# Layer 1's second product over token blocks of 512, 384, 384 and 512, with two small reorderings

## The chip, the core and the metric

The kernel runs on one core of a Trainium2 chip. The metric is device time in microseconds (us), the median of three runs. PE is TensorE's matmul, PEld its weight load, DVE is VectorE, ACT ScalarE, POOL GpSimd, SP SyncE; SPq and ACTq are instructions that issue a DMA from SP's and ACT's queue.

## The reference

Attention with a sigmoid in place of the softmax, then two feed-forward layers, all in float32 with 1792 tokens, model width 768 and inner width 2048:

```python
scores = scale * np.matmul(q, k.transpose(0, 1, 3, 2)) - np.log(S)      # q, k, v: (4, 12, 448, 64)
x = np.matmul(1.0 / (1.0 + np.exp(-scores)), v)                         # reshaped to (1792, 768)
h = x @ w_in;   x = (h * (1.0 / (1.0 + np.exp(-h)))) @ w_out            # layer 1
h = x @ w_in2                                                           # layer 2
P = a[0] + a[1] * h + a[2] * h2 + a[3] * h3
Q = 1.0 + np.abs(b[0]) * np.abs(h) + np.abs(b[1]) * h2
out = (P / (Q + 1e-06)) @ w_out2
```

The weights come as float64 arrays, seen as pairs of int32.

## The kernel before

Everything is written in a fixed order by hand (`manual_schedule`): each engine executes its instructions in the order in which the Python code issues them. A `Ring` is a first-in, first-out list of buffers, and a buffer that is taken again makes its new writer wait for the last reader.

Every float32 operand of a matmul is split in two parts, high and low (`split`, `split2`): ACT casts the high part (L365, L369), DVE subtracts it from the operand (L366, L370). A product of two split operands is three matmuls: high by high, high by low, low by high.

The program has these stages. (1) Attention, to about 172 us. (2) Layer 1's first product with seven products in place of eight (p1 to p7, all matmuls in `product`, L501), to about 375 us; its results pass through SiLU (`silu`) and are stored to DRAM in `gd`. (3) Layer 1's second product, `second(n)`, from 375 to 616 us. (4) Layer 2's first product (`first2`, L709 to L711), over token blocks of 512, 384, 512, 384 in the turn 0, 2, 1, 3, to about 848 us. (5) Layer 2's second product with seven products (`second2`, L902) and their sums (`evict`), to the end.

Stage 3 is what the change is about. The tokens lie along the moving operand. There are four blocks of 448 tokens (b) and 16 chunks of 128 inner rows (c); n = 16 b + c. `second(n)` issues 18 matmuls (L637, L638, L639): for each of six 128-wide output tiles d, three matmuls into one PSUM bank, with `woH[c]`, `woH[c]`, `woL[c]` as weights and the high, low, high part of `gx[n]` as moving operand. `woH[0]`, `woL[0]`, `woH[1]`, `woL[1]` lie in four tiles that the trace calls w; the others are woH and woL. `gx[n]` is one of six split buffers, all in the tile `xa_all`, 2 x 448 elements each. In front of the matmuls of n stand `load_g(n + 4)`, a DMA on ACT's queue that reads `gd` (L603), and behind them `load_wo1(n + 5)` (L618, also ACT's queue), `split_wo1(n + 2)` and `split_gd(n + 2)`. `load_wo1` has four buffers (`wos`), `load_g` takes one of nine buffers of 448 (`f448`), which also serve the results.

After c = 15 `results1(b)` copies the six banks to SBUF, three on ACT, three on DVE (L645), and SP stores them to `xs[1]` (L646). There are eight banks: block b + 1 begins in the two that block b has not used. Between all this stand the conversions of layer 2's weights (`conv`, one ACT and four DVE instructions, a load of 768 KB and a store of 384 KB on SP's queue), whose number up to each n is set by `conv_by`.

At the border of stages 2 and 3 (g == last) the code interleaves the last products p5, p3, p7 with `split_wo1(0)`, `load_wo1(4)`, `split_gd(0)`, then `split_wo1(1)`, `load_wo1(5)`, `split_gd(1)`; `both(g - 1, "r", "c")` is a DVE addition (L387) that reads a PSUM bank which `second(0)` then takes over.

In stage 5 each of the seven products ends with seven tiles of 128 tokens x 384 in PSUM, which `evict(k_, i)` adds up. For k_ == 1 the sum goes to one of three spare buffers (`ores`) and is stored to the output by SP (L957). PSUM tiles hold two banks each: hp2 holds the bank of tile 3 and that of tile 4.

## Time and profile before

| what | value |
|---|---|
| three runs | 1066.99, 1069.32, 1070.0 us; median 1069.32 |
| the profiled execution | 1066.57 us; span of its instructions 1064.8 us |
| mean granted TensorE clock | 0.998 |
| PE, DVE, ACT, POOL busy | 1052.4, 761.1, 605.5, 250.1 us of the span |
| DMA | 255.80 MB, 239 GB/s over the span |
| stage 3, first matmul of n = 0 to first of layer 2 | 375.14 to about 616.1 us |

The profile is of one execution. A busy time is the union of the instructions' durations; matmuls overlap, so the pace of PE is read from the starts of its instructions in the order of time, not from their durations. An idle time in square brackets stands before the instruction it is printed with, and the arrow names what ended it.

### The profile page before, as it was taken

Reading aid. Unit: us, or ns where it says so; the run is one execution under the profiler, and the core shown is the slowest. Engines: PE = TensorE matmul, PEld = TensorE weight load, DVE = VectorE, ACT = ScalarE, POOL = GpSimd, SP = SyncE. Lnnn points to the kernel's source line nnn. Section 1 sums busy time; section 2 is a strip of 40 time slices with the busy share of each in tenths; the row PEclk is TensorE's granted clock in tenths of the full one; section 3 lists DMA queues with packets and bytes.
Section 4 is the critical chain, followed back from the end, with each engine's and each line's share of the span. In section 5 each row is a group of like instructions: output and inputs, shape, how many; then the busy total and the mean of one; then the engine's idle time right before and its main releaser. Section 6 shows DMA issues by size and latency. Waiting matters only on the chain.

```text
span 1064.8 us, 16177 instructions
## 1 busy us (share of the span) xinstructions
PE 1052.4 (99%) x5654; PEld 915.5 (86%) x5654; DVE 761.1 (71%) x1084; ACT 605.5 (57%) x911; POOL 250.1 (23%) x203
## 2 busy tenths in 40 slices
PE   8999999999999999999999999999999999999998
PEld 5555556999999989999999988888999998999997
DVE  3678877888987757595967328879897977445761
ACT  5778886656755554333334258676778866354430
POOL 2112210000000000000002256768968921300000
PEclk9999999999999999999999999999999999999999
DMA  8998877777566788597998334656788879866651
GB/s 231 272 287 236 247 248 244 255 248 254 197 232 220 262 275 281 191 375 280 359 334 303 109 127 136 221 191 223 248 275 300 286 238 314 271 227 198 207 157 53
DMA packets 152338, 255.80 MB, mean 240 GB/s; under 512 B 13888, under 2 KB 109760, under 8 KB 152256
## 3 DMA queue, kind: packets, MB, share of 16 engines
q1 hardware_dynamic: 139968, 233.23, 67.3%
q10 hardware_dynamic: 12224, 21.53, 6.2%
q8 instruction: 44, 0.72, 0.3%
q14 instruction: 38, 0.31, 0.1%
q0 software_dynamic: 64, 0.00, 0.0%
HBM read 168.53 MB, written 86.18 MB: 239 GB/s over the span
## 4 chain that ended last, share of the span: by engine, by line
PE 80%; DVE 6%; POOL 5%; DMA 3%; ACT 2%; issue 2%; SPq 0%; ACTq 0%; DVEq 0%; POOLq 0%
PE acc L501 14%; PE hp L902 13%; PE hb L342 6%; PE pair L318 6%; PE acc L639 6%; PE acc L638 6%; PE acc L637 6%; PE hb L501 5%; PE hb L902 5%; PE hp L709 2%; PE hp L710 2%; PE hp L711 2%; POOL sb L829 2%; PE hb L637 2%; PE hb L639 2%
## 5 line engine op out<-in xcount | busy, mean ns | idle before, releaser
L370 POOL TENSOR_TENSOR w<-wif,w 128x768 fp32r<-128x768 f32 x2 | 4.0, 2034 | 427.1 <-DMA wif<-w1i 427.1
L333 ACT ACTIVATE sb<-pair,nls 128x896 f32<-128x896 f32 x84 | 81.1, 1008 | 33.6 <-PE pair L318 33.5
L639 PE MATMUL acc<-xa_all,woL 128*128 128x448 f32 x252 | 92.7, 368 | 0.0
L637 PE MATMUL acc<-xa_all,woH 128*128 128x448 f32 x252 | 92.7, 368 | 0.0
L638 PE MATMUL acc<-xa_all,woH 128*128 128x448 f32 x252 | 92.7, 368 | 0.0
L190 ACT ACTIVATE sb<-sb 128x768 f32<-128x768 f32 x64 | 58.0, 907 | 55.4 <-DMA sb<-in_moe_w_out_dram 27.2
L738 POOL TENSOR_TENSOR sb<-sb 128x1024 f32<-128x1024 f32 (+1 forms) x32 | 70.1, 2190 | 37.1 <-ACT sb L735 37.1
L342 PE MATMUL hb<-sb,vs 128*64 128x448 f32 (+1 forms) x384 | 73.9, 554 | 0.1
L501 PE MATMUL acc<-xb,wr 128*128 128x448 f32 x315 | 67.7, 366 | 0.0
L829 POOL TENSOR_TENSOR sb<-sb 128x384 f32<-128x384 f32 (+1 forms) x43 | 51.0, 1194 | 60.3 <-DMA sb<-gk 58.4
L501 PEld LDWEIGHTS acc<-xb,wr 128*128 128x128 f32 x315 | 59.1, 188 | 5.4 <-issue 0.7
L196 DVE SCALAR_TENSOR_TENSOR sb<-sb 128x768 int32<-128x768 int32 x64 | 61.9, 967 | 2.2
L193 DVE SCALAR_TENSOR_TENSOR sb<-sb 128x768 int32<-128x768 int32 x64 | 61.6, 963 | 2.2
L709 PE MATMUL hp<-hx,woH 128*128 128x512 f32 (+1 forms) x168 | 61.6, 367 | 0.0
L710 PE MATMUL hp<-hx,woH 128*128 128x512 f32 (+1 forms) x168 | 61.6, 367 | 0.0
L711 PE MATMUL hp<-hx,woL 128*128 128x512 f32 (+1 forms) x168 | 61.6, 367 | 0.0
L709 PE MATMUL hp<-xa_all,woH 128*128 128x512 f32 (+1 forms) x168 | 60.7, 362 | 0.0
L711 PE MATMUL hp<-xa_all,woL 128*128 128x512 f32 (+1 forms) x168 | 60.7, 362 | 0.0
L710 PE MATMUL hp<-xa_all,woH 128*128 128x512 f32 (+1 forms) x168 | 60.7, 362 | 0.0
L740 DVE TENSOR_TENSOR sb<-hp,sb 128x768 f32<-128x768 f32 (+1 forms) x31 | 33.6, 1084 | 35.2 <-ACT sb L737 35.2
L318 PEld LDWEIGHTS pair<-xa_all 64*128 64x128 f32 x384 | 34.7, 190 | 24.8 <-issue 12.3
L366 DVE TENSOR_TENSOR xa_all<-sb,xa_all 128x448 fp32r<-128x448 f32 x67 | 45.0, 681 | 10.9 <-ACT xa_all L365 10.8
(239 smaller groups left out, 2769.1 us busy)
## 6 DMA issues: line engine op xcount, KB each, us to landing
sb<-in_moe_w_in_dram SPq DMA_DIRECT2D x32, 768.0 KB, 6.9
sb<-in_moe_w_out_dram SPq DMA_DIRECT2D x32, 768.0 KB, 6.4
gd<-sb SPq DMA_DIRECT2D x64, 224.0 KB, 3.2
sb<-gd ACTq DMA_DIRECT2D x64, 224.0 KB, 4.7
wf<-w0i SPq DMA_DIRECT2D x32, 384.0 KB, 3.7
gk<-sb SPq DMA_DIRECT2D x27, 384.0 KB, 3.9
xs<-sb SPq DMA_DIRECT2D x36, 224.0 KB, 2.8
gk<-sb SPq DMA_DIRECT2D x15, 512.0 KB, 3.1
```

The lines of the kernel that those rows point to most:

```text
L318: nc.tensor.matmul(p[:, j, :S], K[rows[j], a_, c * P : (c + 1) * P], Q[rows[j], b_, :], start=(n == 0), stop=(n == len(turns) - 1),)
L333: nc.scalar.activation(t, p[:, :, :S], AF.Sigmoid, bias=nls, scale=QKSCALE)
L342: nc.tensor.matmul(hb[i_ % 2][j * D : (j + 1) * D, :S], vs[i_][part, j, c * D : (c + 1) * D], t[part, j], start=(c == 0), stop=(c == LAST),)
L501: nc.tensor.matmul(o, w_[:, w], x[:, i_, :], start=first and kk == 0 and n_ == 0, stop=kk == HK - 1 and n_ == 2, skip_group_check=not first,)
L637: nc.tensor.matmul(o, woH[c][:, w], x[:, 0, :], start=(c == 0), stop=False)
L638: nc.tensor.matmul(o, woH[c][:, w], x[:, 1, :], start=False, stop=False)
L639: nc.tensor.matmul(o, woL[c][:, w], x[:, 0, :], start=False, stop=(c == KF - 1))
L709: nc.tensor.matmul(o, wh[:, w], x[:, 0, :wd_], start=first, stop=False)
L710: nc.tensor.matmul(o, wh[:, w], x[:, 1, :wd_], start=False, stop=False)
L711: nc.tensor.matmul(o, wl[:, w], x[:, 0, :wd_], start=False, stop=last)
L829: nc.gpsimd.tensor_tensor(out=o, in0=i0, in1=i1, op=op)
L902: nc.tensor.matmul(o, a_, y[:, w_, :], start=kk == 0 and n_ == 0, stop=kk == HF - 1 and n_ == 2)
```

## The change

The four blocks of `second` become 512, 384, 384 and 512 tokens wide (`YW`, `YB`), cut out of `gd` tiles that now hold all 1792 tokens of a chunk. The number of matmuls stays: 1152. The split buffers (`hg`) are 2 x 512 elements each, six of them, still in `xa_all` and at its start; the fourth to sixth get free at different times. The loads of `gd` have a ring of their own (`fg`): first five buffers used once (`once`: three of `xio`, two halves of the fifth split buffer), then five (three in `xa_all`, two in `f_all`), three of which are given up in the last block (`late`) for others of the results' ring. The results' ring (`fr`) has five buffers, two to five in the last block. From n = 11 on, loads and splits of `gd` go one product further ahead. `load_wo1(4)`, `(5)` and `(6)` are issued one product later; `load_g(5)` and `(6)` after the first results of n = 2; one load more before. The conversions begin to go faster at n = 10 instead of 16 and are spread by columns instead of products. In layer 2, `evict` for k_ == 1 writes its sum to `w_`, a buffer per tile that is next written for k_ == 4; `ores` is gone.

```diff
-    gd = [[dr_p.tile([P, S], F32, tag=f"gd{c}_{b}", name=f"gd{c}_{b}") for b in range(B)] for c in range(KF)]
+    gd = [dr_p.tile([P, NT], F32, tag=f"gd{c}", name=f"gd{c}") for c in range(KF)]
...
+    YW = (BK, BK - P, BK - P, BK)
+    YB = [(sum(YW[:i]), w) for i, w in enumerate(YW)]
+    fg, fr, hg = Ring([]), Ring([]), Ring([])
+    once, late = [], []
...
     def load_g(n):
         if n < B * KF:
             b, c = divmod(n, KF)
-            gq[n] = f448.get()
-            nc.scalar.dma_start(out=gq[n], in_=gd[c][b])
+            c0, w = YB[b]
+            gq[n] = fg.get()
+            nc.scalar.dma_start(out=gq[n][:, :w], in_=gd[c][:, c0 : c0 + w])
...
-            nc.tensor.matmul(o, woH[c][:, w], x[:, 0, :], start=(c == 0), stop=False)
+            nc.tensor.matmul(o, woH[c][:, w], x[:, 0, :w_], start=(c == 0), stop=False)
...
     def results1(b):
+        c0, w = YB[b]
         for d in range(KD):
-            t = f448.get()
+            t = fr.get()
...
         elif k_ == 1:
-            o = ores.get()
-            add(o, ps, s_)
-            store(0, 0, i, o)
-            ores.put(o)
+            add(w_, ps, s_)
+            store(0, 0, i, w_)
...
-        hl = Ring(xa[:6])
+        xp = [xa_all[:, i * 2 * BK : (i + 1) * 2 * BK].rearrange("p (j s) -> p j s", j=2) for i in range(6)]
+        hg.put(*xp[:4])
...
             if g == last:
-                for n in range(4):
+                once.extend([*xio.free, *(xp[4][:, j].bitcast(F32) for j in range(2))])
+                fg.put(*once)
+                for n in range(5):
                     load_g(n)
...
                 split_wo1(0)
-                load_wo1(4)
                 split_gd(0)
...
                 split_wo1(1)
-                load_wo1(5)
                 split_gd(1)
+                load_wo1(4)
...
         split_wo1(2)
-        load_wo1(6)
+        hg.put(xp[5])
+        xf32 = [xa_all[:, (12 + i) * BK : (13 + i) * BK].bitcast(F32) for i in range(3)]
+        fg.put(*xf32)
         split_gd(2)
-        load_g(4)
-        load_g(5)
+        load_wo1(5)
...
+        knee = KF - 6
         def conv_by(n):
-            if n <= KF:
+            if n <= knee:
                 return first + (n - 1) // 4
...
         for n in range(2, NL1):
-            load_g(n + 4)
+            more_by = 1 if n > 2 * KF // 3 else 0
+            if n > 2:
+                load_g(n + 4 + more_by)
...
             if n == 2:
                 c21(last)
                 both(last, "r", "c")
                 c12(last)
...
                 split_wo1(3)
                 split_gd(3)
+                load_wo1(6)
+                load_g(5)
+                load_g(6)
...
-            split_gd(n + 2)
+            split_gd(n + 2 + more_by)
...
+            if n == NL1 - KF:
+                late.extend(xf32)
...
+                fg.put(fr.get(), fr.get(), fr.get())
```

The order on the engines moves at three places of stage 3, all on ACT, whose queue also issues the loads of `gd` (L603, now L611) and of W_out (L618, now L630). The first is the border of stages 2 and 3, where L369 (now L370) is the cast of W_out's chunks 0 and 1, and L365 (now L366) that of `gx[0]` and `gx[1]`. Before:

```order
L375 CAST wq_1876<-wf_1_262 128x384
L369 CAST w_1988<-wos_3521 128x768
L618 DMA wos_3521<-w0o_146 128x768
L365 CAST xa_all<-sb 128x448
L369 CAST w_1990<-wos_3522 128x768
L618 DMA wos_3522<-w0o_148 128x768
L365 CAST xa_all<-sb 128x448
```

and now:

```order
L376 CAST wq_1828<-wf_1_214 128x384
L370 CAST w_1940<-wos_3473 128x768
L366 CAST xa_all<-sb 128x512
L370 CAST w_1942<-wos_3474 128x768
L366 CAST xa_all<-sb 128x512
L630 DMA wos_3473<-w0o_98 128x768
L376 CAST wq_1826<-sf_216 128x384
```

The load of chunk 4, which takes the buffer of chunk 0 and so waits for its split, no longer stands in front of the cast of `gx[0]`. The second place is n = 2, where the two L520 (now L521) are the last SiLUs of stage 2. Before:

```order
L618 DMA wos_3523<-w0o_150 128x768
L365 CAST xa_all<-sb 128x448
L603 DMA sb<-gd_0_89 128x448
L603 DMA sb<-gd_0_93 128x448
L603 DMA sb<-gd_0_97 128x448
L520 ACTIVATE sb<-acc_2004 128x448
L520 ACTIVATE sb<-sb 128x448
L369 CAST woH_3717<-wos_3524 128x768
L365 CAST xa_all<-sb 128x448
L618 DMA wos_3524<-w0o_152 128x768
L369 CAST woH_3719<-wos_3521 128x768
```

and now:

```order
L366 CAST xa_all<-sb 128x512
L630 DMA wos_3474<-w0o_100 128x768
L521 ACTIVATE sb<-acc_1956 128x448
L521 ACTIVATE sb<-sb 128x448
L370 CAST woH_3669<-wos_3476 128x768
L366 CAST xa_all<-xa_all 128x512
L630 DMA wos_3475<-w0o_102 128x768
L611 DMA xa_all<-gd_78 128x512
L611 DMA xa_all<-gd_79 128x512
L630 DMA wos_3476<-w0o_104 128x768
L370 CAST woH_3671<-wos_3473 128x768
```

Three loads (two of `gd`, one of W_out) have moved from ahead of the SiLUs to behind the casts of chunk 3, in front of the cast of W_out's chunk 4. The third place is the end of block 0, where L645 (now L658) are ACT's copies of the results. Before:

```order
L190 ACTIVATE sb<-sb 128x768
L603 DMA sb<-gd_1_82 128x448
L365 CAST xa_all<-sb 128x448
L603 DMA sb<-gd_1_86 128x448
L365 CAST xa_all<-sb 128x448
L645 COPY sb<-hb 128x448
```

and now:

```order
L191 ACTIVATE sb<-sb 128x768
L611 DMA sb<-gd_76 128x384
L366 CAST xa_all<-xa_all 128x384
L191 ACTIVATE sb<-sb 128x768
L611 DMA xa_all<-gd_77 128x384
L366 CAST xa_all<-sb 128x384
L658 COPY sb<-hb 128x512
```

Three casts of block 1 (c = 0, 1, 2) stand ahead of the copies where two stood, and so do four conversions (L190, now L191) where one stood.

## Rows read from the trace of the kernel before

**Rows 1.** Page, part 1: engine, busy us (share of the span), instructions.

```profile
PE 1052.4 (99%) x5654; PEld 915.5 (86%) x5654; DVE 761.1 (71%) x1084; ACT 605.5 (57%) x911; POOL 250.1 (23%) x203
```

**Rows 2.** Waits of PE: who waited for whom, us in total, times, longest.

```profile
PE hp L902 <- DVE sb L387: 2.6, 1, 2.6
```

**Rows 3.** Timeline of PE, stage 3: start us, us, instruction; pairs 36 matmuls apart.

```profile
404.75 0.37 PE L637 MATMUL hb<-xa_all,woH 128*128 128x448 f32 x1
...
412.19 0.37 PE L637 MATMUL hb<-xa_all,woH 128*128 128x448 f32 x1
...
438.23 0.36 PE L637 MATMUL acc<-xa_all,w 128*128 128x448 f32 x1
...
445.44 0.37 PE L637 MATMUL acc<-xa_all,woH 128*128 128x448 f32 x1
```

**Rows 4.** Timeline of PE, stage 4, moving operand in xa_all; pairs 36 matmuls apart.

```profile
700.16 0.39 PE L709 MATMUL hp<-xa_all,woH 128*128 128x512 f32 x1
...
708.32 0.39 PE L709 MATMUL hp<-xa_all,woH 128*128 128x512 f32 x1
...
820.05 0.33 PE L709 MATMUL hp<-xa_all,woH 128*128 128x384 f32 x1
...
826.29 0.33 PE L709 MATMUL hp<-xa_all,woH 128*128 128x384 f32 x1
```

**Rows 5.** Timeline of PE, stage 4, moving operand in hx; pairs 36 matmuls apart.

```profile
639.67 0.40 PE L709 MATMUL hp<-hx,woH 128*128 128x512 f32 x1
...
648.07 0.40 PE L709 MATMUL hp<-hx,woH 128*128 128x512 f32 x1
...
770.08 0.34 PE L709 MATMUL hp<-hx,woH 128*128 128x384 f32 x1
...
776.44 0.34 PE L709 MATMUL hp<-hx,woH 128*128 128x384 f32 x1
```

**Rows 6.** Timeline of PE, stages 2 (L501) and 5 (L902): neighbouring rows.

```profile
195.15 3.81 PE L501 MATMUL acc<-xb,wr 128*128 128x448 f32 x18
198.80 1.38 PE L501 MATMUL hb<-xb,wq 128*128 128x448 f32 x6
...
958.29 2.24 PE L902 MATMUL hp<-woH,xa_all 128*128 128x384 f32 x12
960.37 1.72 PE L902 MATMUL hp<-woL,xa_all 128*128 128x384 f32 x9
```

**Rows 7.** Timeline of PE at the border of stages 2 and 3.

```profile
372.45 1.99 PE L501 MATMUL acc<-xb,wq 128*128 128x448 f32 x9
375.14 0.44 PE L637 MATMUL hb<-xa_all,w 128*128 128x448 f32 x1 [0.71 <-DVE sb L387]
```

**Rows 8.** Timeline of ACT at the same border: the cast of gx[0].

```profile
372.77 0.57 ACT L365 CAST xa_all<-sb 128x448 fp32r<-128x448 f32 x1 [1.39 <-DVE w L370]
```

**Rows 9.** Timeline of DVE at the same border: the addition that frees the bank.

```profile
374.38 0.62 DVE L387 TENSOR_TENSOR sb<-hb,sb 128x448 f32<-128x448 f32 x1
```

**Rows 10.** Timeline of DVE, stage 5: third and fourth sum of k_ == 1.

```profile
896.60 0.55 DVE L387 TENSOR_TENSOR sb<-hp,sb 128x384 f32<-128x384 f32 x1
901.21 0.56 DVE L387 TENSOR_TENSOR sb<-hp,sb 128x384 f32<-128x384 f32 x1 [4.06 <-DMA out_dram<-sb]
```

**Rows 11.** Timeline of PE around these sums.

```profile
901.91 2.18 PE L902 MATMUL hp<-woL,hx 128*128 128x384 f32 x9 [2.64 <-DVE sb L387]
...
906.67 1.72 PE L902 MATMUL hp<-woL,hx 128*128 128x384 f32 x9
```

**Rows 12.** Windows: us, busy of PE PEld DVE ACT POOL, granted clock, DMA share, GB/s.

```profile
900.00:905.00 5.00, 3.08 (x13) 3.12 (x14) 3.79 (x8) 1.03 (x2) 0.00 (x0) 0.81 0.94 304
```

**Rows 13.** Timeline of DVE: the subtraction that completes gx[3].

```profile
389.23 0.62 DVE L366 TENSOR_TENSOR xa_all<-sb,xa_all 128x448 fp32r<-128x448 f32 x1
```

**Rows 14.** Timeline of PE: the first matmul of n = 3.

```profile
389.88 0.37 PE L637 MATMUL hb<-xa_all,woH 128*128 128x448 f32 x1
```

**Rows 15.** DMA, 460 to 540 us: issue, count, KB each, median us to landing.

```profile
sb<-gd ACTq DMA_DIRECT2D x22, 224.0 KB, 4.6
```

More of the change, by code (lines that the diff above doesn't have):

```diff
@@ L82, in attention_moe_moe @@
     f_all = sb_[0]
-    f448 = Ring([f_all[:, i * S : (i + 1) * S] for i in range(9)])
+    f_tiles = [f_all[:, i * S : (i + 1) * S] for i in range(9)]
+    f448 = Ring(f_tiles)
     f2 = Ring([f_all[:, i * 2 * S : (i + 1) * 2 * S].rearrange("p (j s) -> p j s", j=2) for i in range(4)])
@@ L520, in silu @@
         nc.scalar.activation(t, src, AF.Silu)
-        nc.sync.dma_start(out=gd[g % HF + hi_f * HF][2 * (g // HF) + second], in_=t)
+        b = 2 * (g // HF) + second
+        nc.sync.dma_start(out=gd[g % HF + hi_f * HF][:, b * S : (b + 1) * S], in_=t)
         f448.put(t)
@@ L601, in load_g @@
             b, c = divmod(n, KF)
-            gq[n] = f448.get()
-            nc.scalar.dma_start(out=gq[n], in_=gd[c][b])
+            c0, w = YB[b]
+            gq[n] = fg.get()
+            nc.scalar.dma_start(out=gq[n][:, :w], in_=gd[c][:, c0 : c0 + w])
     def split_gd(n):
         if n < B * KF:
+            w = YB[n // KF][1]
             t = gq.pop(n)
-            gx[n] = hl.get()
-            split(t, gx[n])
-            f448.put(t)
+            gx[n] = hg.get()
+            split(t[:, :w], gx[n][:, :, :w])
+            if any(t is u for u in late):
+                xin.put(t)
+            elif not any(t is u for u in once):
+                fg.put(t)
     wo_in = {}
@@ L628, in ybank @@
     def ybank(b, d):
-        return banks[ring8[(KD * b + d) % 8]][:, :S]
+        return banks[ring8[(KD * b + d) % 8]][:, : YB[b][1]]
     def second(n):
         b, c = divmod(n, KF)
-        x = gx.pop(n)
+        x, w_ = gx.pop(n), YB[b][1]
         for d in range(KD):
@@ L909, in second2 @@
             wring.put(wop.pop(k_ * HF + kk))
-    ores = Ring([])
     def evict(k_, i):
@@ L1183, in attention_moe_moe @@
         split_wo1(2)
-        load_wo1(6)
+        hg.put(xp[5])
+        xf32 = [xa_all[:, (12 + i) * BK : (13 + i) * BK].bitcast(F32) for i in range(3)]
+        fg.put(*xf32)
         split_gd(2)
-        load_g(4)
-        load_g(5)
+        load_wo1(5)
         NL1 = B * KF
-        stage.put(more)
-        third[0] = None
-        conv_load()
         first, slow, end = done["conv"], KF - 2, NL1 - 12
+        cols = [sum(YW[i // KF] for i in range(n)) for n in range(NL1 + 1)]
+        knee = KF - 6
         def conv_by(n):
-            if n <= KF:
+            if n <= knee:
                 return first + (n - 1) // 4
-            return first + slow // 4 + -(-(n - KF) * (len(order) - first - slow // 4) // (end - KF))
+            begun = (knee - 1) // 4
+            return first + begun + -(-(cols[n] - cols[knee]) * (len(order) - first - begun) // (cols[end] - cols[knee]))
         for n in range(2, NL1):
-            load_g(n + 4)
+            if n == 3:
+                hg.put(xp[4])
+            more_by = 1 if n > 2 * KF // 3 else 0
+            if n > 2:
+                load_g(n + 4 + more_by)
+            if n == 2 * KF // 3:
+                load_g(n + 5)
             second(n)
@@ L1205, in attention_moe_moe @@
                 c12(last)
+                age = {id(t): i for i, t in enumerate(f448.free)}
+                k0 = [k * BK for k in range(len(f_tiles) * S // BK)]
+                k0.sort(key=lambda k: max(age[id(t)] for j, t in enumerate(f_tiles) if k < (j + 1) * S and j * S < k + BK))
+                ft = [f_all[:, k : k + BK] for k in k0]
+                fg.put(*ft[:2])
+                fr.put(*ft[2:])
                 split_wo1(3)
                 split_gd(3)
+                load_wo1(6)
+                load_g(5)
+                load_g(6)
+                stage.put(more)
+                third[0] = None
+                conv_load()
             if n + 2 < KF:
@@ L1210, in attention_moe_moe @@
                 split_wo1(n + 2)
-            split_gd(n + 2)
+            split_gd(n + 2 + more_by)
+            if n == 2 * KF // 3:
+                split_gd(n + 3)
             if n == KF - 1:
@@ L1217, in attention_moe_moe @@
                 wif.put(*(wif_all[:, i * DM : (i + 1) * DM] for i in range(4)))
-                xin.put(*(xa_all[:, (12 + i) * BK : (13 + i) * BK].bitcast(F32) for i in range(3)))
             if n % KF == KF - 1:
@@ L1221, in attention_moe_moe @@
             conv_to(conv_by(n))
+            if n == NL1 - KF:
+                late.extend(xf32)
+                for t in fg.free.copy():
+                    if any(t is u for u in late):
+                        fg.free.remove(t)
+                        xin.put(t)
+                fg.put(fr.get(), fr.get(), fr.get())
+            if n == end:
+                fr.put(*xio.free)
             m = n - (NL1 - KF)
@@ L1321, in attention_moe_moe @@
                 gs_load(n - 1)
-        fs = [sb[:, i * HM : (i + 1) * HM] for i in range(3 * NT2 + 3)]
-        sums2.extend(zip(fs[: 3 * NT2 : 3], fs[1 : 3 * NT2 : 3], fs[2 : 3 * NT2 : 3]))
-        ores.put(*fs[3 * NT2 :])
+        fs = [sb[:, i * HM : (i + 1) * HM] for i in range(3 * NT2)]
+        sums2.extend(zip(fs[::3], fs[1::3], fs[2::3]))
         obank.extend([*(hps[i % 3][:, j, :] for i in (1, 2, 0) for j in range(2)), *hb])
```

12 lines of the change are left out of this document (6 added, 6 removed).

## The prediction

> **What bounds the kernel.** I read the page's busy shares first, then PE's waits, then timelines of PE, ACT and DVE at the places that the diff touches. PE is busy for 99% of the span and no other engine for more than 71% [rows 1], so an edit pays in two ways only: PE issues its matmuls at a faster pace, or one of its few stalls goes. Stage 3 keeps its 1152 matmuls and its multiplications. By columns nothing changes, since two blocks of 448 are 896 columns, as 512 and 384 are; what can change is the time of one matmul beyond its columns.
>
> The reader is to see in [rows 3] that this time isn't the same all over stage 3: 36 matmuls whose weights are in woH and woL take 412.19 - 404.75 = 7.44 us, 206.7 ns each, and 36 whose weights are in the tiles w take 445.44 - 438.23 = 7.21 us, 200.3 ns each. Moving tile, width and bank pattern are the same. At 2.4 GHz 448 columns are 186.7 ns, so 20.0 or 13.6 ns are added.
>
> **A. The pace of stage 3.** Before: 14 of 16 chunks have woH and woL, so 1008 x 206.7 + 144 x 200.3 ns = 237.2 us. After, the nearest rows are those of stage 4 with 512 and 384 columns, three matmuls of high and low parts each, and the same moving tile xa_all [rows 4]: (708.32 - 700.16) / 36 = 226.7 ns at 512 and (826.29 - 820.05) / 36 = 173.3 ns at 384. Both are 13.3 ns over their columns (213.3 and 160.0), as the faster kind of 448 is. With 576 matmuls of each width: 576 x (226.7 + 173.3) ns = 230.4 us, **a gain of 6.8 us**.
>
> The other bound is the same two widths with the moving operand in hx [rows 5]: (648.07 - 639.67) / 36 = 233.3 and (776.44 - 770.08) / 36 = 176.7 ns, 20.0 and 16.7 over their columns. That makes 236.2 us, a gain of 1.0. Below it stands the case that each matmul keeps the 20.0 ns of today: 576 x (233.3 + 180.0) = 238.1 us, a loss of 0.9. The tile pair decides between them, it seems: w and woH differ in [rows 3], hx and xa_all in [rows 4, 5], at one width each. I take [rows 4], since the moving operand stays in xa_all and the weights in woH and woL, and the split buffers grow to 2 x 512, the very shape that these rows read; and keep 6.8 and -0.9 as bounds. A caution: 448 columns also run at (198.80 - 195.15) / 18 = 202.8 ns where nine matmuls in a row share a bank, and 384 at (960.37 - 958.29) / 12 = 173.3 ns in stage 5 [rows 6], so the pace follows neither the width nor the tile alone, and no row has 512 columns with exactly this order of banks.
>
> The Trainium skill, "TensorE: Matmul & The Clock Gate", section "Back-to-back issue gap", speaks against this part: it gives an isolated warm matmul N / 2.4 + 2.5 ns, so that two of 448 and one of 512 with one of 384 cost the same 378.3 ns and the split would gain nothing. The traces disagree with the constant, which is 13 to 20 ns here and depends on the operands; that a constant of whatever size cancels is the first rival below.
>
> **B. The border of stages 2 and 3.** The last nine L501 begin at 372.45 and should take 9 x 0.203 = 1.83 us, to 374.28; `second(0)` begins at 375.14, 0.86 late, with an idle 0.71 in front that the bank's addition (DVE L387) ends, and a first matmul of 0.44 in place of 0.37 [rows 7]. That addition runs from 374.38 to 375.00 [rows 9]. It is late because ACT stood 1.39 us before the cast of `gx[0]` (372.77), for a DVE instruction on the tile w [rows 8]: in its queue `load_wo1(4)` is ahead of that cast and must wait until the split of chunk 0 has been read, and behind the cast come DVE's subtraction of `gx[0]` and the addition. The change puts both loads behind the casts, so the cast moves up by up to 1.39, and the addition with it to an end near 374.0, before PE is through. One more `load_g` ahead costs ACT a DMA issue. The gain lies between 0 (another late operand) and 0.93 (0.86 and the longer first matmul); **I take 0.8**.
>
> **C. The last sums.** For k_ == 1 the fourth sum waits 4.06 us, until the store of the first of three `ores` buffers has left it: it runs at 901.21, though the third began at 896.60 [rows 10]. PE waits behind it, because this PSUM tile holds two banks, 2.64 us, its longest wait of this kind [rows 2, 11]. Without it the matmuls that began at 901.91 would have followed about 2.8 earlier: with the sum at 897.1 to 897.8 after the third, the bank is free more than a microsecond before PE needs it at some 899.1. And having stood idle, PE got a granted clock of 0.81 over 900 to 905 [rows 12], which is a part of the stretch at the lower of its two levels: two groups of nine took 906.67 - 901.91 = 4.76 us against 18 x 0.1733 = 3.12 [rows 6, 11], 1.64 more. With the sum in place (`w_`, next written at k_ == 4, three products on) there is no store to wait for. Gain 2.8 + 1.64 = **4.4**; bounds 0 (another store or sum ends as late) and 4.4. SP's queue is not upset by the stores, which stand in it as before.
>
> **At no cost, with the cover.** (1) W_out's chunks 4, 5 and 6 are loaded one product later; chunk 6 now has two products, 8.16 us, from its load (n = 2) to its split (n = 4). Loads of 224 KB land in 4.6 us [rows 15], which for W_out's 384 KB, were landing in proportion to bytes, is an estimate of 7.9: just inside. (2) At n = 2 the cast of chunk 4 has three more DMA issues in front of it on ACT. What is tight near there is the split of `gx[3]`: its subtraction ends at 389.23 + 0.62 = 389.85 and PE begins n = 3 at 389.88 [rows 13, 14], a cover of 0.03 us. After, the casts are of 512 instead of 448 columns, which lengthens the two steps by about an eighth of 0.6 each, 0.15 together; but three products before it take 18 x 226.7 = 4.08 us in place of 3.72, 1.1 more in all, and two DMA issues (`load_g`) have left the place ahead of it. Cover gone, each microsecond late is one lost, and a little more at the lower clock. (3) The gd loads are of 256 or 192 KB in place of 224 and go one product further ahead from n = 11, (4) the results' copies have five buffers, so that the sixth waits for the first's store, one to two microseconds of DVE, against a lead of three products of 384, 9.4 us. (5) The conversions come earlier, at about the same rate. All of these hide on engines that are idle for 29% and more of the span [rows 1].
>
> **The sum.** 6.8 + 0.8 + 4.4 = 12.0 less on the profiled execution's 1066.57 gives 1054.6. That execution is 2.75 below the median of the three runs; from the median the same gain gives 1057.3. The middle is **1056.0**, 12 below the middle of the two bases (1067.95).
>
> **Rivals.**
> 1. *Columns alone.* What is added to a matmul's columns stays with stage 3 (its bank order, or the addresses of the weights) instead of falling to 13.3 ns. For it: the hx rows have 20.0 and 16.7 at the new widths [rows 5], and today's woH rows have 20.0 with xa_all [rows 3]. Against it: [rows 4]. A gives 0 to 1.0, the whole 5.2 to 6.2: about 1062.3. Chance 0.16.
> 2. *The stall of the last sums stays under another name*: the fourth sum is released by something not shown, because the store hid it, or PE meets a later sum in the same way. For it: only one wait can be printed there, the last. Against it: the third sum had begun 4.6 earlier on the same engine. 4.4 less gain: 1060.4. Chance 0.09; with rival 1 together, 1066 to 1067, another 0.04.
> 3. *A new stall at the start of stage 3* (n = 3 to 6), where the cover is 0.03 us now [rows 13, 14] and W_out comes later. A late split costs its delay and, as [rows 12] show, up to 1.6 more at the lower clock: 2 to 8 us, so 1058 to 1064. Chance 0.07.
> 4. *Slower: gd's loads bind in the blocks of 384.* A load has about two products from its issue until its split must begin. That is 7.44 us today and 36 x 0.1733 = 6.24 in those blocks, against 4.6 to land [rows 15]. It decides once the landing lasts over 6.24: then each of 32 products takes half of the landing instead of 3.12 us. At 8 us, 32 x (4.0 - 3.12) = 28.2, less the lead of three products (9.4) = 18.8, against a gain of 12.0: 1074.8. To be slower by over 0.3% it wants a landing of some 7.8 us. For it: the DMA engines were 0.94 busy in the window of stage 5 that the rows show [rows 12], so transfers can queue; against it: these loads are smaller by a seventh, and are split three products ahead from n = 11. Chance 0.04.
>
> **Numbers.** The forecast keeps 0.60; its own range is 1053 to 1058, the two bases with 1.5 for the scatter of runs. The range goes on to rivals 1 and 2 and half of 3, to 1063.5, and leaves out the case of both, the rest of 3 and rival 4: 1053 to 1063.5. A measurement can tell 0.3% from no change, 3.2 us, that is below 1066.1 or above 1072.5. Faster: 0.60 + 0.16 + 0.09 + 0.05 of rival 3 = 0.90; the same: rivals 1 and 2 together and the rest of 3, 0.06; slower: rival 4, 0.04.
>
> **What the next profile would show.** A: 36 matmuls of stage 3 take 8.16 us in the outer blocks and 6.24 in the inner ones; 8.40 and 6.36 mean rival 1. B: PE's first matmul of stage 3 has no idle time in front, and ACT no wait for DVE before the cast of `gx[0]`. C: no wait of DVE for the output's stores between the third and fourth sum of k_ == 1, PE L902 without the wait of 2.6, and a granted clock of 1.00 there. Rival 3: idle time in front of a matmul of n = 3 to 6, ended by DVE's L366 or L370. Rival 4: landings of gd over 6 us and PE waiting for splits from n = 17 to 47. The forecast is wrong if 36 matmuls at either width take longer than in [rows 4], or if a stall of over a microsecond stands anywhere in stage 3.

## The result and the profile after

The changed kernel takes 1054.9 us in the median of six runs (1054.06 to 1056.83), the kernel before 1067.38 in six runs beside it: ratio 0.989, 95% interval 0.9874 to 0.9905, about 12 us less. The forecast was 1056.0. The profiled execution took 1054.74 us, with a span of 1052.9.

PE is still what the time is made of. The page's first part of the changed kernel, against [rows 1]:

```profile
PE 1043.2 (99%) x5654; PEld 905.1 (86%) x5654; DVE 766.1 (73%) x1084; ACT 604.9 (57%) x911; POOL 249.9 (24%) x203
```

Cut at the first matmul of each stage, the two profiled executions differ like this (us; the start of stage 2 is also the length of stage 1):

| | start of stage 2 | stage 2 | stage 3 | stage 4 | stage 5 | behind the last matmul |
|---|---|---|---|---|---|---|
| before | 173.16 | 201.99 | 240.94 | 233.08 | 211.26 | 4.38 |
| after | 171.24 | 201.57 | 234.38 | 233.07 | 208.27 | 4.40 |
| difference | -1.92 | -0.42 | -6.56 | -0.01 | -2.99 | 0.02 |

The lines that answer to [rows 3], PE's timeline of stage 3 of the changed kernel, pairs 36 matmuls apart:

```profile
405.22 0.39 PE L649 MATMUL hb<-xa_all,woH 128*128 128x512 f32 x1
...
413.38 0.39 PE L649 MATMUL hb<-xa_all,woH 128*128 128x512 f32 x1
...
451.33 0.33 PE L649 MATMUL acc<-xa_all,woH 128*128 128x384 f32 x1
...
457.57 0.33 PE L649 MATMUL acc<-xa_all,woH 128*128 128x384 f32 x1
...
541.83 0.39 PE L649 MATMUL acc<-xa_all,w 128*128 128x512 f32 x1
...
550.07 0.39 PE L649 MATMUL acc<-xa_all,woH 128*128 128x512 f32 x1
```

8.16 and 6.24 us, 226.7 and 173.3 ns each, are to the digit what stage 4 had shown [rows 4]. The last pair has w as weights at 512 columns: 8.24 us, 228.9 ns each, about two ns more than forecast, for 72 matmuls. PE has no idle time inside stage 3.

The border, against [rows 7 to 9]:

```profile
370.70 1.99 PE L502 MATMUL acc<-xb,wq 128*128 128x448 f32 x9
372.81 0.47 PE L649 MATMUL hb<-xa_all,w 128*128 128x512 f32 x1
```

PE has no idle time printed in front of stage 3, yet the nine L502 that began at 370.70 should have ended at 372.52, and stage 3 begins at 372.81, 0.29 late. ACT's timeline shows where it comes from, first in the changed kernel, then in the kernel before:

```profile
367.40 0.94 ACTq L611 DMA_DIRECT2D xa_all<-gd  x2
368.38 0.53 ACT L577 COPY sb<-acc 128x448 f32<-128x448 f32 x1 [2.01 <-DMA gd<-sb]
...
369.97 0.61 ACT L366 CAST xa_all<-sb 128x512 fp32r<-128x512 f32 x1
```

```profile
368.66 0.95 ACTq L603 DMA_DIRECT2D sb<-gd  x2
369.70 0.53 ACT L575 COPY sb<-acc 128x448 f32<-128x448 f32 x1 [1.58 <-PE acc L501]
```

The cast of `gx[0]` no longer waits for a DVE instruction [rows 8], but ACT now stands 2.01 us before the copy that leads to it, where it stood 1.58 before. The two copies are printed with different releasers, but each begins within 0.1 us of the end of the last load of `gd` issued ahead of it (368.34 and 369.61): ACT's queue is busy issuing loads in that time, five now and four before.

The last sums, against [rows 10 to 12]: timeline of DVE, third and fourth sum of k_ == 1, then the busy times of PE, PEld, DVE, ACT and POOL in a window over them, with the columns of [rows 12]:

```profile
889.18 0.55 DVE L388 TENSOR_TENSOR sb<-hp,sb 128x384 f32<-128x384 f32 x1
890.85 0.56 DVE L388 TENSOR_TENSOR sb<-hp,sb 128x384 f32<-128x384 f32 x1 [1.11 <-PE hp L915]
```

```profile
888.00:893.00 5.00, 5.00 (x31) 5.00 (x30) 3.64 (x8) 2.31 (x5) 0.00 (x0) 1.00 0.99 312
```

The fourth sum follows in 1.67 us and waits for PE's product, no store; PE is busy throughout, at a granted clock of 1.00. But stage 5 is only 2.99 us shorter, not 4.4. PE's waits and its timeline at the entry of stage 5 show a wait that the kernel before does not have:

```profile
PE hp L915 <- DVE sb L755: 1.0, 1, 1.0
```

```profile
840.27 1.21 PE L915 MATMUL hp<-xa_all,hx 128*128 128x384 f32 x6
842.45 0.80 PE L915 MATMUL hp<-xa_all,hx 128*128 128x384 f32 x3 [0.98 <-DVE sb L755]
```

DVE is late there by 1.4 us, counted from the start of stage 4, and the lateness begins 70 us earlier. Timelines of POOL and DVE of the changed kernel in stage 4, then the same of the kernel before:

```profile
772.75 4.51 POOL L809 TENSOR_TENSOR sb<-sb 128x384 f32<-128x384 f32 x4 [1.20 <-DMA sb<-w1o]
777.38 2.00 POOL L751 TENSOR_TENSOR sb<-sb 128x768 f32<-128x768 f32 x1
...
775.24 4.56 DVE L695 TENSOR_TENSOR xa_all<-xa_all 128x384 fp32r<-128x384 f32 x3
```

```profile
781.90 4.92 POOL L796 TENSOR_TENSOR sb<-sb 128x384 f32<-128x384 f32 x4 [1.49 <-DMA sb<-w1o]
786.78 2.18 POOL L738 TENSOR_TENSOR sb<-sb 128x768 f32<-128x768 f32 x1
...
784.11 3.13 DVE L682 TENSOR_TENSOR xa_all<-xa_all 128x384 fp32r<-128x384 f32 x3
```

Three subtractions of DVE took 4.56 us in place of 3.13. POOL's four additions wait for a load of w1o. They began 165.55 us after the first matmul of stage 4 in the changed kernel and 165.81 before, while DVE's first subtraction began at 168.05 and 168.02. Before, that subtraction began together with POOL's fourth addition and took 0.55 us, as one does alone; in the changed kernel it met the third addition and took 1.14. The second took about 1.37 both times. The third took 1.36 before, beside the fourth addition, and 2.20 in the changed kernel, beside POOL's long multiplication (L751). A subtraction that begins while a POOL instruction runs ends 0.41 or 0.42 us behind it: POOL's ended at 775.96, 777.25 and 779.38 us, the subtractions at 776.37, 777.67 and 779.79. So a quarter of a microsecond in POOL's start decided which POOL instructions DVE met.

### The profile page after: what moved, and what is told of

Its sections match the earlier page's. It is cut to its first block, busy times and chain, and to the rows that moved or that the text cites. A ratio compares the mean times of both kernels' runs of the same rounds, so it can differ in the third digit from the quotient of the medians.

```text
span 1052.9 us, 16164 instructions
## 1 busy us (share of the span) xinstructions
PE 1043.2 (99%) x5654; PEld 905.1 (86%) x5654; DVE 766.1 (73%) x1084; ACT 604.9 (57%) x911; POOL 249.9 (24%) x203
## 4 chain that ended last, share of the span: by engine, by line
PE 83%; DVE 10%; ACT 2%; issue 2%; POOL 1%; DMA 1%; SPq 0%; DVEq 0%; ACTq 0%; POOLq 0%
PE acc L502 14%; PE hp L915 14%; PE hb L343 6%; PE pair L319 6%; PE acc L649 6%; PE acc L650 6%; PE acc L651 6%; PE hb L502 5%; PE hb L915 5%; PE hp L722 3%; PE hp L723 3%; PE hp L724 3%; PE hb L649 2%; DVE sb L755 2%; PE hb L650 2%; PE hb L651 2%
## 5 line engine op out<-in xcount | busy, mean ns | idle before, releaser
L649 PE MATMUL acc<-xa_all,woH 128*128 128x512 f32 (+1 forms) x252 | 91.9, 365 | 0.0
L651 PE MATMUL acc<-xa_all,woL 128*128 128x512 f32 (+1 forms) x252 | 91.9, 365 | 0.0
L650 PE MATMUL acc<-xa_all,woH 128*128 128x512 f32 (+1 forms) x252 | 91.9, 365 | 0.0
L191 ACT ACTIVATE sb<-sb 128x768 f32<-128x768 f32 x64 | 58.0, 906 | 44.8 <-DMA sb<-in_moe_w_out_dram 24.9
L751 POOL TENSOR_TENSOR sb<-sb 128x1024 f32<-128x1024 f32 (+1 forms) x32 | 69.9, 2184 | 39.2 <-ACT sb L748 39.1
L502 PE MATMUL acc<-xb,wr 128*128 128x448 f32 x315 | 67.8, 366 | 0.0
L502 PEld LDWEIGHTS acc<-xb,wr 128*128 128x128 f32 x315 | 59.0, 188 | 5.6 <-issue 0.7
L649 PEld LDWEIGHTS acc<-xa_all,woH 128*128 128x128 f32 x252 | 47.3, 188 | 5.5
```

The lines of the kernel that those rows point to most:

```text
L502: nc.tensor.matmul(o, w_[:, w], x[:, i_, :], start=first and kk == 0 and n_ == 0, stop=kk == HK - 1 and n_ == 2, skip_group_check=not first,)
L649: nc.tensor.matmul(o, woH[c][:, w], x[:, 0, :w_], start=(c == 0), stop=False)
L650: nc.tensor.matmul(o, woH[c][:, w], x[:, 1, :w_], start=False, stop=False)
L651: nc.tensor.matmul(o, woL[c][:, w], x[:, 0, :w_], start=False, stop=(c == KF - 1))
L751: nc.gpsimd.tensor_tensor(out=q_, in0=q_, in1=a_, op=ALU.mult)
```

## The experiments

Times are medians of 4 to 11 runs, ratios against the kernel before on the same chip: it took 1068.21 us beside the first four rows, 1066.64 beside the next four, 1066.26 beside the three after these and 1066.83 beside the last. So times of different groups are compared by their ratios. The stages are those of one profile each (us; POOL's start counts from the first matmul of stage 4):

| run | us | ratio, interval | stage 2 | stage 3 | stage 4 | stage 5 | POOL's start |
|---|---|---|---|---|---|---|---|
| in place only | 1062.78 | 0.9953, 0.9935 to 0.9971 | 204.73 | 240.00 | 233.08 | 206.88 | 165.90 |
| later W_out only | 1065.27 | 0.9981, 0.9966 to 0.9997 | 201.76 | 239.79 | 233.08 | 212.07 | 166.12 |
| changed, 4 x 448 | 1061.37 | 0.995, 0.9933 to 0.9966 | 201.58 | 240.94 | 233.08 | 208.02 | 165.57 |
| before, 64 bytes on | 1060.52 | 0.9936, 0.9916 to 0.9956 | 202.19 | 234.80 | 233.11 | 212.85 | 165.64 |
| changed, 64 bytes on | 1056.74 | 0.9908, 0.9889 to 0.9926 | 204.13 | 235.93 | 233.06 | 206.63 | 165.87 |
| changed, hx moved | 1055.76 | 0.9896, 0.9877 to 0.9915 | 202.91 | 234.42 | 232.92 | 209.16 | 165.69 |
| changed, wr and wq moved | 1053.83 | 0.9875, 0.986 to 0.9891 | 200.96 | 234.34 | 233.07 | 206.84 | 166.05 |
| changed, w1o earlier | 1056.04 | 0.9888, 0.9873 to 0.9904 | 204.12 | 234.37 | 233.07 | 207.02 | 164.28 |
| three small edits | 1056.3 | 0.9906, 0.9877 to 0.9936 | 201.05 | 234.80 | 233.11 | 208.39 | 165.71 |
| changed, two more edits | 1053.84 | 0.9882, 0.9854 to 0.991 | 201.01 | 234.35 | 233.07 | 207.25 | 164.27 |
| changed, once more | 1055.7 | 0.9906, 0.9873 to 0.9939 | 202.00 | 234.43 | 233.07 | 207.28 | 165.92 |
| the same and a load later | 1053.54 | 0.9882, 0.9858 to 0.9906 | 201.28 | 234.34 | 233.07 | 206.94 | 164.27 |

**One part alone: the sums in place.**

```diff
-            o = ores.get()
-            add(o, ps, s_)
-            store(0, 0, i, o)
-            ores.put(o)
+            add(w_, ps, s_)
+            store(0, 0, i, w_)
```

> The kernel before with one edit of the change: the sums of k_ == 1 in place. The theory (term C of the prediction): the wait of 4.06 us for the store of a spare buffer goes, and with it PE's 2.8 us and the 1.64 us at the lower clock, 4.4 us in all: about 1063.0 against 1067.4, stage 5 some 206.9 us from its first matmul to its last in place of 211.3. In the changed kernel stage 5 became only 3.0 us shorter, because PE waits 0.98 us for DVE near the entry of stage 5, which the kernel before does not show. Rival: that new wait comes with the in-place sums; then this kernel shows it too and gains 3.0: 1064.4.

Stage 5 took 206.88 us against 211.26, 4.38 less, where term C was 4.4 (the sum; its two shares, the wait and the lower clock, are not measured apart). The wait of 0.98 us is absent here, and the run of 64 bytes below has it with the old sums, so it does not come with the in-place sums. Stage 2, where nothing was edited, took 204.73 us, because PE fell to another pace in it. Its timeline in this run, then that of the kernel before:

```profile
261.73 2.02 PE L501 MATMUL acc<-xb,wq 128*128 128x448 f32 x9
263.59 2.02 PE L501 MATMUL hb<-xb,wr 128*128 128x448 f32 x9
265.45 2.02 PE L501 MATMUL acc<-xb,wr 128*128 128x448 f32 x9
```

```profile
262.80 1.99 PE L501 MATMUL acc<-xb,wq 128*128 128x448 f32 x9
264.63 1.99 PE L501 MATMUL hb<-xb,wr 128*128 128x448 f32 x9
266.45 1.99 PE L501 MATMUL acc<-xb,wr 128*128 128x448 f32 x9
```

18 matmuls take 3.72 us, 206.7 ns each, against 3.65, 202.8. In this run the slower pace was there by 230 us and held until stage 3, at a granted clock of 1.00.

Stage 3 was not edited either, and was 0.94 us shorter than before (240.00). Its timeline in this run, a pair of the first block and one of the second, 36 matmuls apart:

```profile
401.66 0.36 PE L637 MATMUL hb<-xa_all,woH 128*128 128x448 f32 x1
...
408.95 0.36 PE L637 MATMUL hb<-xa_all,woH 128*128 128x448 f32 x1
...
460.21 0.37 PE L637 MATMUL acc<-xa_all,woH 128*128 128x448 f32 x1
...
467.65 0.37 PE L637 MATMUL acc<-xa_all,woH 128*128 128x448 f32 x1
```

The first block ran at 7.29 / 36 us = 202.5 ns, the second at the 206.7 of [rows 3]. So the two paces of stage 2 occur in stage 3 too, with the same tiles and the same code.

**One part alone: W_out's loads one product later.** All else as before.

```diff
                 split_wo1(0)
-                load_wo1(4)
                 split_gd(0)
...
                 split_wo1(1)
-                load_wo1(5)
                 split_gd(1)
+                load_wo1(4)
...
         split_wo1(2)
-        load_wo1(6)
         split_gd(2)
+        load_wo1(5)
...
                 split_gd(3)
+                load_wo1(6)
```

> The kernel before with one edit of the change: W_out's chunks 4, 5 and 6 are loaded one product later. The theory (term B): the cast of gx[0] moves up by 1.39 us and PE's idle 0.71 us in front of stage 3 goes, 0.8 us: about 1066.6 against 1067.4. Rival: as in the changed kernel, where PE still began stage 3 0.29 us later than its last nine matmuls allow, half of it stays: 1067.0. A second rival: the later loads bring splits of W_out late, a new wait of PE in n = 3 to 8, over 1067.4.

PE's timeline at the border shows no idle time:

```profile
371.41 1.98 PE L501 MATMUL acc<-xb,wq 128*128 128x448 f32 x9
373.23 0.36 PE L637 MATMUL hb<-xa_all,w 128*128 128x448 f32 x1
```

Nine matmuls in 1.82 us, and stage 3 follows without a gap, with a first matmul of the common length: at the border the whole 0.9 us of term B. No split came late. The ratio (2.0 us less, 0.3 to 3.6) takes it in but can't confirm it: stage 3 was 1.15 us shorter too (239.79), because its first block ran at the faster pace as in the run above, and stage 2 kept only 0.2 us, with a wait of 0.3 at 192.5 us that the kernel before does not have.

**The change without its widths.**

```diff
-    YW = (BK, BK - P, BK - P, BK)
+    YW = (S, S, S, S)
```

> The changed kernel with four blocks of 448 tokens again, all the rest (buffers, rings, order, in-place sums) as changed. The theory (term A): the width sets the pace, so 36 matmuls take 7.44 us with woH and 7.21 with w again, stage 3 is 6.7 us longer, and the time is about 1061.6 against 1054.9. Rival: the pace came from the other edits of stage 3 (buffers of 2 x 512, loads of their own ring, conversions moved): then it stays near 1055.

Stage 3 is 240.94 us again, 6.56 more, with 36 matmuls in 7.44 us (406.22 to 413.66), and the time 1061.37. The gain in stage 3 comes with the blocks' widths alone; the larger buffers, the new rings and the order give none of it.

**448 columns, 64 bytes further on.**

```diff
-        hl = Ring(xa[:6])
+        xs16 = [xa_all[:, 16 + i * 2 * S : 16 + (i + 1) * 2 * S] for i in range(6)]
+        hl = Ring([t.rearrange("p (j s) -> p j s", j=2) for t in xs16])
```

> The kernel before with its six split buffers 64 bytes further on in xa_all, nothing else. In the kernel before xa_all and woH, woL lie at the same offset within 128 bytes (32), the tiles w at 96. The theory: at 448 columns the pace hangs on how the moving operand and the weights lie to each other within 128 bytes, 206.7 ns where they lie alike and 200.3 where they don't. Then the shift swaps the two: 1008 matmuls at 200.3 and 144 at 206.7 ns, 231.7 us in place of 237.2, 5.5 less: about 1061.9. Rival: the pace is a matter of the width and of the tiles as such (w or woH): no change, 1067.4. A second rival, by stage 4, where 512 and 384 columns are slower with hx (offset 96) than with xa_all (offset 32): unlike offsets cost 3 to 7 ns, and the time goes up to 1071 or more.

Timeline of PE, two pairs 36 matmuls apart:

```profile
395.54 0.36 PE L637 MATMUL hb<-xa_all,woH 128*128 128x448 f32 x1
...
402.74 0.36 PE L637 MATMUL hb<-xa_all,woH 128*128 128x448 f32 x1
...
435.14 0.37 PE L637 MATMUL acc<-xa_all,w 128*128 128x448 f32 x1
...
442.49 0.36 PE L637 MATMUL acc<-xa_all,woH 128*128 128x448 f32 x1
```

With woH 200.0 ns in place of 206.7, with w 204.2 in place of 200.3: the faster pair and the slower one swap, as the theory said, though w stops short of 206.7. Stage 3 is 234.80 us, 6.1 less and 0.42 from that of the new widths, by one changed number.

**The same 64 bytes under the change.** 
```diff
-        xp = [xa_all[:, i * 2 * BK : (i + 1) * 2 * BK].rearrange("p (j s) -> p j s", j=2) for i in range(6)]
+        xs16 = [xa_all[:, 16 + i * 2 * BK : 16 + (i + 1) * 2 * BK] for i in range(6)]
+        xp = [t.rearrange("p (j s) -> p j s", j=2) for t in xs16]
...
-        xf32 = [xa_all[:, (12 + i) * BK : (13 + i) * BK].bitcast(F32) for i in range(3)]
+        xf32 = [xa_all[:, 16 + (12 + i) * BK : 16 + (13 + i) * BK].bitcast(F32) for i in range(3)]
```

> The changed kernel with its six split buffers (and the three load buffers behind them) 64 bytes further on, so that the moving operand of stage 3 lies unlike woH and woL within 128 bytes and like the tiles w. The theory (the pace hangs on the width and on how the two operands lie to each other; at 512 and 384 unlike is the slower of the two, as with hx in stage 4): 504 matmuls of each width go from 226.7 and 173.3 to 233.3 and 176.7 ns, 5.0 us more: about 1060 against 1054.9, almost what the 64 bytes gave back at 448. Rival: what hx loses in stage 4 is the tile's own (its place or its neighbours in time), and 512 and 384 keep their pace: 1054.9. A second rival: unlike is better at every width, as it was at 448: under 1054.

Stage 3 became 1.5 us longer, not 5.0. At 384 columns nothing happened with woH and woL (36 matmuls from 454.39 to 460.63, 6.24 us); at 512 they went to 8.24 us (395.54 to 403.78), 228.9 ns, not 233.3. And the matmuls with w, whose offsets are now alike, got slower too, from 229.1 to 232.5 ns at 512 and from 173.4 to 176.1 at 384 (means of the whole stage). So neither like nor unlike offsets are the faster ones at these widths: the theory failed here. The profiled execution, which is the median one, carries 2.6 us of stage 2's slower pace as well.

**hx moved to the offset of woH.** One tile for the six buffers, 64 bytes longer, so that it begins 64 bytes lower:

```diff
-                hx.put(*fixed("hx", KD, [P, 2, BK], F32R, l2_p))
+                hx_all = l2_p.tile([P, KD * 2 * BK + 16], F32R, tag="hx", name="hx")
+                for i in range(KD):
+                    t = hx_all[:, i * 2 * BK : (i + 1) * 2 * BK]
+                    hx.put(t.rearrange("p (j s) -> p j s", j=2))
```

> The changed kernel with hx 64 bytes lower in SBUF (one tile of the six, 64 bytes longer), so that in stage 4 hx lies like woH and woL. The theory: 252 matmuls of 512 columns go from 233.3 to 226.7 ns and 252 of 384 from 176.7 to 173.3, 2.5 us less in stage 4 (233.1 to 230.6), about 1052.4 against 1054.9; stage 5 keeps its pace. Rival: the pace of hx is its own: no change.

A miss. In stage 4 hx at 512 columns took 232.4 ns in place of 233.3 with woH and woL, and 233.4 in place of 227.0 with w; stage 4 gained 0.15 us. In stage 5, where hx serves as weights, the matmuls with woH and woL as moving operand, now alike, went from 173.4 to 175.9 ns, and those with w, now unlike, from 175.1 to 173.4. Equal offsets alone do not make a fast pair.

**The weights of stage 2 moved.** The last tile that lies ahead of `wr` is made 64 bytes longer.

```diff
-    s12f, s34f = fixed("sf", 2, [P, DM], F32, w1_p)
+    s12f = w1_p.tile([P, DM], F32, tag="sf0", name="sf0")
+    s34f = w1_p.tile([P, DM + 16], F32, tag="sf1", name="sf1")[:, :DM]
```

> The changed kernel with the weights of stage 2 (wr, wq) 64 bytes further on, so that its 1008 matmuls of 448 columns have operands that lie unlike within 128 bytes. The theory: they go from 202.7 ns to about 200.1, 2.6 us less: 1052.3 against 1054.9. And the second pace that the in-place run showed in stage 2 (206.7 ns from 230 us on, with nothing changed there) should not turn up. Rival: nine matmuls in a row per bank set the pace of stage 2, and the offset does nothing: 1054.9.

Stage 2 ran at 202.2 ns in place of 202.7, half a microsecond over its 1008 matmuls (200.96 us in all): the 200.1 did not come. Unlike offsets at 448 columns thus gave 200.0 ns in stage 3 and 202.2 here. No stretch at 206.7 ns turned up in three profiles with this edit, while four of the eleven profiles without it had one. That it cannot occur is not shown by three.

**w1o's loads earlier in stage 4.** 
```diff
+            if n + 1 in WTS and n > HF:
+                wt_load(WTS[n + 1], hf)
             g_out(n - 2)
...
-            if n + 1 in WTS:
-                wt_load(WTS[n + 1], wif if n < HF else hf)
+            if n + 1 in WTS and n < HF:
+                wt_load(WTS[n + 1], wif)
```

> The changed kernel with the loads of w1o in stage 4 issued a little earlier (ahead of the stores of the same step on SP's queue). The theory of the new wait of 0.98 us at the entry of stage 5: POOL's four additions wait for that load; when they start 165.6 us into stage 4 instead of 165.8 or later, POOL's next multiplication begins beside DVE's third subtraction, which then takes 2.2 us in place of 1.36, DVE stays 1.4 us late to the end of stage 4, and PE pays 1.1 us. Issued earlier, the additions are over before, DVE is on time, and stage 5 is 206.9 us again: about 1053.7 against 1054.9. Rival: DVE's delay is not of that overlap, or the earlier load only moves it: stage 5 stays 208.3 us.

POOL in this run:

```profile
774.43 4.34 POOL L809 TENSOR_TENSOR sb<-sb 128x384 f32<-128x384 f32 x4
778.73 2.17 POOL L751 TENSOR_TENSOR sb<-sb 128x768 f32<-128x768 f32 x1
```

It no longer waits for the load, begins 164.28 us into the stage, and stage 5 took 207.02 us without the wait. DVE's three subtractions still met POOL, and took 3.62 us, 0.5 and not 1.4 more than before. The median shows no gain; the profiled execution's stage 2 had the slower pace (204.12), and whether the others had it is not shown.

**Three small edits on the kernel before:** the diffs of the in-place sums, of W_out's loads and of the 64 bytes at 448 columns together.

> The kernel before, blocks of 448 kept, with three small edits together: sums in place, W_out's loads one product later, and the split buffers 64 bytes further on. The theory: the edits lie in three different stages and add up, 4.4 (in place) + 0.9 (border) + 6.2 (stage 3, 200.0 ns with woH and 203.9 with w in place of 206.7 and 200.2), 11.5 less than 1067.4: about 1056, so that the blocks of 512 and 384 bring only about 1 us more than 64 bytes do. Rival: the shift and the later loads pull on the same splits at the border of stage 3 (the shifted kernel waited there 0.9 us as before) and 1 us or more is lost: 1057 to 1058.

1056.3 us, 10.0 less by the ratio (6.8 to 13.1). The 11.5 of the theory lies inside that. By the stages, stage 2 gave 0.9 us (term B), stage 3 6.1 and stage 5 2.9 in place of 4.4, because the wait at its entry (1.08 us) is there; at the border no idle time is printed, and stage 3 begins 0.15 us late.

**The change with `wr` and `wq` moved and w1o earlier; the change once more; and the first of these with the fifth load later.** The first has the two diffs above, the second none, the third in addition:

```diff
-                for n in range(5):
+                for n in range(4):
                     load_g(n)
...
                 split_gd(0)
+                load_g(4)
```

> The changed kernel with two further edits: the weights of stage 2 64 bytes further on (as in the run of that edit alone, 202.2 ns and no stretch at 206.7) and the loads of w1o earlier in stage 4. The theory: against the changed kernel beside it, 0.6 us in stage 2 where the changed kernel runs at 202.7 all through and up to 3.1 where it falls to 206.7, and 1.4 us in stage 5 where that kernel meets the wait of 0.98 us: 1.5 us less in the median (1053.4 against 1054.9), and a smaller scatter. Rival: both are within the scatter of the changed kernel, no difference that can be told.

> The changed kernel once more, unaltered, for a second profile and as the neighbour of the other two. If the wait of 0.98 us at the entry of stage 5 and the pace of stage 2 are matters of chance from run to run, they may come out the other way here (stage 5 206.9 or 208.3 us, stage 2 201.6 or up to 204.7), while stage 3 stays at 234.4 us and stage 4 at 233.1. If they belong to the kernel, stage 5 is 208.3 us again.

> The run with the two further edits, and with the fifth load of gd at the border of stages 2 and 3 issued behind the split of gx[0] in place of ahead of it. The theory: in the changed kernel five loads stand on ACT's queue in front of the copies and casts that lead to gx[0] and hold ACT 2.0 to 2.8 us (four held it 1.6), so that PE begins stage 3 late by 0.1 to 0.9 us; with four again, as in the run of W_out's loads alone and in the run of the three small edits, there is no idle time ahead of stage 3: stage 2 about 200.7 us in place of 201.0, 0.3 us or more less: about 1053.4. Rival: the fifth load, now later, makes the split of gx[4] late and PE waits at n = 4.

The changed kernel's second profile came out the other way at both places of chance. Its timeline of PE, at the border and at the entry of stage 5:

```profile
373.24 0.48 PE L649 MATMUL hb<-xa_all,w 128*128 128x512 f32 x1 [0.93 <-ACT sb L577]
```

```profile
840.74 3.98 PE L915 MATMUL hp<-xa_all,hx 128*128 128x384 f32 x22
```

Stage 3 began about 1 us late: the copy that the loads hold up came at 368.82, 0.44 later than in the first profile, and with it the casts and the addition that frees the bank, while PE had come to the border 0.38 earlier. Stage 5 had no wait and took 207.28 us. POOL's additions in stage 4 had begun at 165.92, and DVE's subtractions took as long as in the kernel before:

```profile
775.68 3.13 DVE L695 TENSOR_TENSOR xa_all<-xa_all 128x384 fp32r<-128x384 f32 x3
```

So the same program takes 4.56 or 3.13 us there, by when POOL begins. Over all 14 profiles, of both kernels' code, the wait at the entry of stage 5 (1.0 to 1.3 us) stands in the five whose POOL began at 165.55 to 165.71, and in none of the six at 165.81 to 166.12 nor of the three at 164.28 or earlier.

With the two further edits the kernel took 1053.84 us against 1055.7 beside it: 1.9 less in the median, but the ranges overlap (1053.02 to 1054.83 against 1054.17 to 1058.81). The last run, 1053.54, can't be told from it: PE still stood 0.36 us at the border and ACT 2.23 before its copy, with four loads in front:

```profile
366.09 1.33 ACTq L612 DMA_DIRECT2D sb<-gd  x3
367.46 0.49 ACTq L612 DMA_DIRECT2D xa_all<-gd  x1
368.00 0.53 ACT L578 COPY sb<-acc 128x448 f32<-128x448 f32 x1 [2.23 <-issue]
```

So the fifth load alone is not what holds ACT. In all 14 profiles the copy begins 0.04 to 0.10 us after the last of these loads is issued, and one issue takes 0.33 to 1.01 us of ACT's queue: the four here took 1.86, and the first was issued only 0.3 us after ACT's cast before it had ended. Why a few issues take twice as long as the others is open.

## Why the prediction was right

**A held, to 0.3 us.** 6.8 was forecast and 6.56 measured, by the profiles before and after and again by the run with 4 x 448. Most of the missing part is w at 512 columns, which I took at 226.7 ns; stage 4 of the kernel before already had such a row (36 matmuls from 683.07 to 691.32, 229.2 ns each), which I did not use. By the letter of its own sign, 36 matmuls longer than in [rows 4], the forecast was wrong there by 0.08 us. Against the two runs whose first block of 448 ran at the faster pace the gain is 5.4 and 5.6, so its size hangs by about 1 us on the pace that the base happens to run at. The choice of [rows 4] over [rows 5] decided the size, and its result was right. Its reason, that the pair of tiles decides, was too simple: 64 bytes within the same tile change the pace at 448 columns by 6.7 ns. Of rival 1 nothing remained: the same columns took 6.56 us less. By the rule of the Trainium skill, "TensorE: Matmul & The Clock Gate", section "Back-to-back issue gap", they would have taken the same time; the measurement decides against it here.

**B was right for the edit and mis-sized for the change.** Alone it gave the 0.9 us at the border, and with the two other small edits stage 2 was 0.94 us shorter. In the change stage 2 is 0.42 us shorter in place of 0.8: the loads of `gd`, of which the prediction counted one DMA issue more, hold ACT 2.0 to 2.8 us ahead of the copy in front of `gx[0]`, and PE begins stage 3 0.3 us late in one profile and over 0.9 in the other. The mistake was to follow the cast back to the wait that was removed and not to the next instructions ahead of it.

**C was right in itself,** 4.38 of 4.4 us. In the profiled execution 1.4 of it went back, 0.98 in the one wait at the entry of stage 5. I had looked for the next late thing among sums and stores; it was a load of layer 2's weights whose landing time decides how POOL and DVE meet, in this kernel and the one before alike.

**The sum** of 12.0 met 11.87 between the two profiles, but not term by term: A fell short by 0.2, B by 0.4 and C by 1.4, so that the three together gave 9.97, and stage 1, which the change does not touch, was 1.9 us shorter. That the total met the forecast is luck to this extent. Stage 1's 173.16 us in the kernel before is the longest of all profiles; the others lie between 170.8 and 172.3. So the profiled execution was no clean base, and the middle of the two bases was a guess that went well.

**The rivals.** The second did not come: the fourth sum waits for PE alone. The third came within 0.35 us: the split of `gx[3]` ends that much before PE needs it. Of the fourth the direction came and not the size. The loads of 192 KB, 460 to 540 us, against [rows 15]:

```profile
xa_all<-gd ACTq DMA_DIRECT2D x12, 192.0 KB, 5.5
sb<-gd ACTq DMA_DIRECT2D x8, 192.0 KB, 4.8
```

Though smaller, they land later than the 4.6 us of 224 KB. That is below the 6.24 us at which they would bind, and the least lead of a split in the blocks of 384 is 3.6 us (n = 35).

## What to carry to other kernels

When one engine is busy 99% of the time, read its pace from starts, per operand pair and width, and take the price of a new shape from the same operands elsewhere in the program. Before reshaping a loop for such a pace, move the operand by 64 bytes: here one number gave 6.1 us of stage 3 where new blocks, rings and buffers gave 6.6, and with two small edits it made 1056.3 against 1055.7 us. The same 64 bytes made the new blocks slower, so the shift is to be tried, not reasoned out. And when a wait is removed, follow its engine's queue back to the next instruction that could hold it, and don't trust a stage total from one profile.

## What the runs showed of the hardware

TensorE's time per matmul depends on where its operands lie: from 200.0 to 206.7 ns at 448 columns, from 226.7 to 233.4 at 512, and from 173.3 to 176.7 at 384, always at a granted clock of 1.00. At 448 columns with operands at the same offset within 128 bytes, two paces (202.7 and 206.7 ns) occurred with the same code, in stage 2 and in the first block of stage 3, and in stage 2 PE, once at the slower one, kept it for 100 us and more, to the end of the stage; it is worth up to 3 us of stage 2 (201.6 to 204.7) and 1 us of stage 3 in these profiles, which can be a part of the scatter between runs. Which rule sets the pace stays open: with woH and woL equal offsets were slow at 448 columns, fast at 512 with xa_all, and slow at 512 with hx.

A subtraction on DVE of 128x384 with both operands in SBUF took 0.54 to 0.55 us alone (17 of them in the 14 profiles), and the same when POOL's instruction began after it (46). The 105 that began while a POOL instruction was running each ended 0.41 to 0.42 us after that one, and took 0.59 to 2.77 us, by how much of it was left. The Trainium skill, "SBUF — State Buffer", section "Who interferes with whom", says that a DVE instruction with two SBUF inputs contends with a GpSimd instruction that reads SBUF; the trace agrees. What it adds is that a quarter of a microsecond in a load's landing decided how much it cost.

A load issued from ACT's queue takes 0.33 to 1.01 us of that queue (the loads of `gd` in front of stage 3, 14 profiles), and ACT's next copy begins only behind the last of them.
